# Two heads' outputs in the spare rows of the others: an output projection on three and a half row tiles instead of four

## The chip, the cores and the metric

One Trainium2 chip, one of its cores. The metric is the device time of one execution in microseconds (us); the kernel before took 1962.9 us (median of three runs, 1961.62 to 1962.97).

## The reference

Two kinds of layers alternate, twice each, on x of shape 1 x 2048 x 448 in float32:

```python
def _A_ref(x, wq, wk, wv, wo):        # attention, 16 heads of 28, one key and value for all heads
    q = (x @ wq).reshape(B, S, H, Dh).transpose(0, 2, 1, 3)
    k = x @ wk
    v = x @ wv
    scores = jnp.einsum("bhqd,bkd->bhqk", q, k) * (Dh ** -0.5)
    p = _softmax(scores, axis=-1)
    o = jnp.einsum("bhqk,bkd->bhqd", p, v)
    return o.transpose(0, 2, 1, 3).reshape(B, S, H * Dh) @ wo

def _B_ref(x, w_gate, w_up, w_down):  # feed-forward, F = 1792
    return (_silu(x @ w_gate) * (x @ w_up)) @ w_down

x = x + _A_ref(_layernorm(x), ...)
x = x + _B_ref(_layernorm(x), ...)
x = x + _A_ref(_layernorm(x), ...)
x = x + _B_ref(_layernorm(x), ...)
```

The change lies in the last product of `_A_ref`, (2048 x 448) @ (448 x 448), and in the hand-over from the first `_B_ref` to the second `_A_ref`.

## The kernel before

**Tiles.** The residual x stays in SBUF as `xres`, 16 tiles of 128 rows. The 2048 rows are worked on in four chunks of 512 (c = 0 to 3). Operands of most products are cut in a high and a low part (`split`: high on POOL by a rounding copy, low as the rest), and a product is made of three: high by high, high by low, low by high.

**Attention.** `GR` lists 16 passes i, one for each chunk c and group g of four heads, and each pass has 16 key tiles kt, so the loop in `Attention.scores` runs n = 16 i + kt over 256 steps. `step(n)` makes the scores of four heads at once, on four row strips of the array, 32 rows each (28 of them a head's own): three heads into three banks of PSUM (`three`), the fourth into one of the banks 6 and 7 (`one`, chosen by `single`). ScalarE makes the exponentials (L638 to L644); in odd steps the fourth head goes through a copy on VectorE (L640). After each odd step `pv` multiplies the two steps before by the values and VectorE adds into an accumulator (L679, L682).

**Layout of a group's output.** The four heads of a group lie one above the other, 32 rows each: 28 of the head's own, one with the sum of its softmax, three of zeros. So a group fills 128 rows and only 112 carry output.

**Post-processing.** Three pairs of steps after a pass has ended, at kt = 5 of the next pass, `rest` runs: VectorE takes the reciprocal of the sums, SyncE writes it to DRAM and reads it back spread over the rows (L703, L704), POOL multiplies (L711) and splits into `onh` and `onl` (L139, L140 in the helper `split`).

**Output projection.** When the fourth group of chunk 0, 1 or 2 is done, `between`, called after each odd step, runs `outproj` at the next kt = 10: for each of the chunk's four row tiles 4 groups x 3 products of full height (L614), then one addition into `xres` on VectorE (L618). Tiles 0 and 1 use two of the three banks in `free`, tiles 2 and 3 banks 6 and 7. The last chunk's projection is made after the loop, between two units of the feed-forward. `load_wo(z)`, at kt = 8 of passes 2 and 3, loads the output weights in the same layout: 28 rows of 32 for each head, the other four cleared by POOL.

**What else runs in passes 4c + 5.** The table `later` puts the next layernorm of a chunk into the pass that follows its projection: four statistics at kt 0 to 3, the reciprocal root on POOL at kt 4 (L246, L247), then per row tile one application (L255) and one transposition (L260) on VectorE; the transposed chunk goes to DRAM and comes back through `load`. At kt = 8 of passes 11 to 13 the weights of the first feed-forward blocks are loaded into the tile `wr` and split on POOL; `wr` has one buffer, which `load_wo` uses too.

**Order.** Each engine works through its instructions in the order in which the program issues them, SyncE's transfers and POOL's operations among them (`manual_schedule`), so a waiting instruction holds back all behind it on its engine.

**Hand-over.** In the last feed-forward block of layer 0, `hand_over` prepares the next attention. Chunk 0 is normalised, sent to DRAM and loaded back transposed into `xn`, a tile with one buffer, and `cut` splits it. Chunk 1's `ready` applies its norm into the same `xn`; it is queued by `soon` behind three calls of `project`. TensorE then transposes it (`flip`, L296). `unit` runs the lists in `mid` between its matmuls, those in `soon` near its end.

Of the kernel before, what the change touches and what calls it, by code (L numbers as in the profile page):

```python
# [52 lines left out]
def forward(  # L53
# [84 lines left out]
    def split(hi, lo, raw):  # L138
        nc.gpsimd.tensor_scalar(hi, raw, 1.0, 0.0, ALU.mult, ALU.add)  # L139
        nc.gpsimd.tensor_tensor(lo, raw, hi, ALU.subtract)  # L140
# [93 lines left out]
    def norm_steps(c, away=None, n=1):  # L234


        got = {}

        def stat(t):
            nc.vector.bn_stats(stats[:, 4 * c + t, :], xres[:, 4 * c + t, :])  # L240
            nc.vector.bn_aggr(mv[:, 4 * c + t, :], stats[:, 4 * c + t, :])

        def scale(z):
            m = 4 // n
            rstd = pers.tile([P, 4], F32, name="rstd", bufs=2)[:, 0:m]
            nc.gpsimd.tensor_scalar(rstd, mv[:, 4 * c + m * z : 4 * c + m * z + m, 1], 1.0, EPS, ALU.mult, ALU.add)  # L246
            nc.gpsimd.tensor_tensor(rstd, rstd, halfn[:, 0:m], ALU.pow)  # L247
            got["r"] = got.get("r", []) + [rstd[:, t : t + 1] for t in range(m)]

        def apply(t):  # L250
            if t == 0:
                got["x"] = pers.tile([P, 4, 512], F32, name="xn")
            got["o"] = (away() if away else got["x"][:, t, :])[:, 0:D]
            i, r = xres[:, 4 * c + t, :], got["r"][t]
            nc.vector.tensor_scalar(got["o"], i, mv[:, 4 * c + t, 0:1], r, ALU.subtract, ALU.mult)  # L255
            if not away:
                nc.gpsimd.tensor_copy(got["x"][:, t, D:512], got["o"][:, 384:D])

        def turn(t):
            nc.vector.transpose(side()[:, :, :, t], got["o"].rearrange("p (k s) -> p k s", s=32))  # L260

        def side():
            return got["x"].rearrange("p t n -> p (t n)")[:, 0 : 4 * D].rearrange("p (k s t) -> p k s t", s=32, t=4)

        def send():
            turns.append(dram.tile([D, 512], F32, name=f"xt{len(turns)}"))
            got["xt"] = turns[-1]
            for a in range(4):
                nc.sync.dma_start(
                    got["xt"].rearrange("(k r) n -> r k n", r=32)[:, :, P * a : P * a + P],  # L270
                    side()[32 * a : 32 * a + 32].rearrange("p k s t -> p k (s t)"),
                )

        def load():
            got["raw"] = pers.tile([P, 4, 512], F32, name="xn")
            rows3(got["raw"], got["xt"])

        got["load"] = load
        fs = [lambda t=t: stat(t) for t in range(4)] + [lambda z=z: scale(z) for z in range(n)]
        for t in range(4):  # L280
            fs += [lambda t=t: apply(t)] + [lambda t=t: turn(t)] * bool(away)
        return fs + [send] * bool(away), got
# [3 lines left out]
    def cut(got, tiles, ks=range(4), copy=nc.scalar.copy):  # L286

        for k in ks:
            flipped(tiles, k, got["raw"][:, k, :], copy)

    def flip(got, tiles, ks=range(4)):

# [68 lines left out]
    class Attention:  # L361
# [230 lines left out]
        def scores(self, ff):  # L592
            next(switch)
            with tc.tile_pool(name=f"at{self.layer}", bufs=1, reuse_waits="tile") as wp:
# [3 lines left out]
                todo, due = [], {}  # L598
                single = lambda d: banks[6 + d % 2]

                def load_wo(z):
                    r = wpool.tile([P, 4, 2, P], F32, name="wr").rearrange("p (z k) b n -> p z (k b n)", z=2)
                    nc.gpsimd.memset(r, 0.0)
                    for j in range(4):
                        nc.sync.dma_start(r[32 * j : 32 * j + DH, :, 0:D], wos[j][:, 2 * z : 2 * z + 2, :])
                    zs = slice(2 * z, 2 * z + 2)
                    split(woh[:, zs, :], wol[:, zs, :], r[:, :, 0:D])

                def outproj(c, t, po, gs=range(NG)):
                    oh, ol = on[c]  # L610
                    ts_ = slice(P * t, P * t + P)
                    for g in gs:
                        for z, (a, b) in enumerate(((oh, woh), (oh, wol), (ol, woh))):
                            nc.tensor.matmul(  # L614
                                po[:, 0:D], a[:, g, ts_], b[:, g, :], start=(g + z == 0), stop=(g == NG - 1 and z == 2)
                            )
                    if gs[-1] == NG - 1:
                        return lambda: nc.vector.tensor_tensor(  # L618
                            xres[:, 4 * c + t, :], po[:, 0:D], xres[:, 4 * c + t, :], ALU.add
                        )  # L620
# [26 lines left out]
                def between(d):  # L647

                    i, kt = divmod(2 * d, NT)
                    free, one = threes[0], single(d + 1)  # L650
                    if full:
                        self.lent = free[:, 0, :]
                        if 6 <= kt < 14:
                            self.advance(min(NM // 4, NM * (i + 2) - self.done))
                        if kt == 14 and i + 1 < len(GR):
                            self.places[i + 1](free[:, 1, :])
                    if not todo or kt != 10:
                        return
                    c = todo.pop()
                    for f in [outproj(c, t, free[:, t, :]) for t in range(2)]:  # L660
                        f()
                    outproj(c, 2, one)()
                    outproj(c, 3, single(d))()

                def pv(d):

# [19 lines left out]
                def post(i):  # L686

                    c, g = GR[i]
                    out2 = accs.pop(i)
                    oraw, rb = out2[:, 0, :], out2[:, 1, :]  # L690
                    rs = wp.tile([P, 16], F32, name="rs", bufs=2)
                    for j in range(4):
                        nc.sync.dma_start(rs[32 * j : 32 * j + 32, :], oraw[32 * j + DH : 32 * j + DH + 1, :])

                    def rest():
                        if fine is not None:
                            under = wp.tile([P, 16], F32, name="under", bufs=2)
                            for bound, op in ((LIMIT, ALU.is_lt), (1.0 / LIMIT, ALU.is_gt)):
                                nc.vector.tensor_scalar(under, rs, bound, None, op)
                                nc.vector.tensor_tensor(fine, fine, under, ALU.mult)  # L700
                        nc.vector.reciprocal(rs, rs)
                        rd = dram.tile([4, 512], F32, name="rd", bufs=2)
                        nc.sync.dma_start(rd.rearrange("j (p n) -> (j p) n", n=16), rs)  # L703
                        nc.sync.dma_start(rb, rd[:, None, :].to_broadcast([4, 32, 512]))  # L704
                        if g == 0:
                            on[c] = (
                                wp.tile([P, NG, 512], F32R, name="onh"),
                                wp.tile([P, NG, 512], F32R, name="onl"),
                            )
                        oh, ol = on[c]  # L710
                        nc.gpsimd.tensor_tensor(rb, oraw, rb, ALU.mult)  # L711
                        split(oh[:, g, :], ol[:, g, :], rb)
                        if g == NG - 1 and c < NC - 1:
                            todo.append(c)

                    return rest
# [16 lines left out]
                for n in range(last):  # L733
# [5 lines left out]
                    if kt == 12 and i + 2 < len(GR):  # L739
                        self.stack(i + 2)  # L740
                    if i in (2, 3) and kt == 8:
                        load_wo(i - 2)
                    if n == NT and ff.nxt:
                        ff.nxt.below(nc.sync)
                    if kt == 8 and 10 < i <= 11 + FG:
# [37 lines left out]
    class FeedForward:  # L783
# [251 lines left out]
        def hand_over(self, gi, c):  # L1035

            a = self.nxt
            fs, got = norm_steps(c, None if c else lambda: qraw)
            for f in fs[:5]:
                f()  # L1040
            a.pool = self.stage
            a.X[c] = xtile(xpool if c < 2 else self.xbp)

            def ready():
                for f in fs[5:]:
                    f()
                a.norms[c] = got

            wipe = lambda: nc.gpsimd.memset(qraw, 0.0)
            if c == 0:  # L1050
                self.soon.append([1, lambda: [f() for f in fs[5:9]]])
                self.soon.append([2, lambda: [f() for f in (*fs[9:], got["load"], wipe)]])
                self.mid[gi, 3, 1] = [lambda: None, lambda: cut(got, a.X[c])]
                self.soon.append([5, lambda: [a.project() for _ in range(3)]])
            elif c == 1:
                self.soon.append([3, ready])
            else:
                a.plan[4 * c - 4, 0] = [ready]

# [254 lines left out]
```

## Time and profile before

| | |
|---|---|
| median of three runs | 1962.9 us (1961.62 to 1962.97) |
| profiled execution, its own time | 1962.7 us |
| its span (first to last instruction) | 1960.9 us |
| granted TensorE clock | 1.00 |
| TensorE matmuls, busy | 1947.1 us, 99% |
| VectorE / ScalarE / GpSimd, busy | 1016.9 / 1339.3 / 771.3 us |
| DMA | 79.69 MB, mean 41 GB/s |
| matmuls of the output projection (L614) | 384, of which 288 in the six projections inside the loop |

In the rows below PE is TensorE's matmuls, PEld its weight loads, DVE VectorE, ACT ScalarE, POOL GpSimd, SP SyncE; SPq is a transfer issued from SyncE's queue. A row of a timeline has the start in us, the time taken, engine, line, operation, the tiles written and read, and how many were merged into the row; in brackets how long the engine had been idle before it and what ended that. A row of several merged instructions spans from the first's start to the last's end.

### The profile page before, as it was taken

What the parts mean: (1) busy time and instruction counts of PE and PEld (TensorE: products, weight loads), DVE (VectorE), ACT (ScalarE), POOL (GpSimd) and SP (SyncE); (2) the same over time, 40 slices, a digit from 0 to 9 for tenths busy, and PEclk for the clock granted to TensorE, in tenths of its full rate; (3) what the DMA queues carried; (4) which work ended last, traced back from release to release, by engine and by line L of the source; (5) the groups of instructions that cost most, each with busy time, mean ns of one, the idle gap of its engine ahead of it and who ended that gap; (6) DMA issues with size and microseconds to landing.
All of it is one profiled execution on the core that took longest, in us unless ns stands there. A gap on an engine that the chain in (4) does not pass through costs nothing. (4 is left out here: it accounts for less than half of the span.)

```text
span 1960.9 us, 45644 instructions
## 1 busy us (share of the span) xinstructions
PE 1947.1 (99%) x18307; PEld 1319.9 (67%) x18307; DVE 1016.9 (52%) x1711; ACT 1339.3 (68%) x2353; POOL 771.3 (39%) x997
## 2 busy tenths in 40 slices
PE   9999999999999999999999999999999999999998
PEld 8544545445458999999974444454444688999997
DVE  7434543544435567665654335435444346667653
ACT  4899797998964344444349998979979533444432
POOL 5212111132314868766341221111222167688640
PEclk9999999999999999999999999999999999999999
DMA  5111020121210110011131111102112101110102
GB/s 168 53 30 26 25 49 20 32 59 28 73 33 2 53 33 24 24 33 27 52 112 33 29 31 31 45 12 61 31 50 50 33 6 49 33 32 22 27 17 77
DMA packets 100001, 79.69 MB, mean 41 GB/s; under 512 B 26024, under 2 KB 82984, under 8 KB 99784
## 3 DMA queue, kind: packets, MB, share of 16 engines
q1 hardware_dynamic: 99208, 75.81, 14.3%
q8 instruction: 144, 2.36, 0.5%
q10 hardware_dynamic: 576, 0.92, 0.1%
q14 instruction: 73, 0.60, 0.1%
HBM read 57.15 MB, written 18.74 MB: 39 GB/s over the span
## 5 line engine op out<-in xcount | busy, mean ns | idle before, releaser
L672 PE MATMUL bank<-pt,vsb 128*32 128x512 f32 x4096 | 493.3, 598 | 0.3
L631 PE MATMUL bank<-qstack,keys 32*128 32x512 f32 x1536 | 484.7, 425 | 0.0
L631 PE MATMUL three<-qstack,keys 32*128 32x512 f32 x4608 | 460.6, 425 | 1.5 <-DVE vt L565 1.2
L631 PEld LDWEIGHTS three<-qstack,keys 32*128 32x128 f32 x4608 | 254.4, 182 | 295.0 <-ACT pt L644 179.4
L638 ACT ACTIVATE pt<-three 128x1536 f32<-128x1536 f32 x256 | 372.1, 1454 | 1.2 <-PE bank L672 0.8
L644 ACT ACTIVATE pt<-three 128x1536 f32<-128x1536 f32 x256 | 371.7, 1452 | 0.0
L350 PE MATMUL bank<-xh,wgh 64*128 64x512 f32 x1344 | 364.5, 392 | 0.3 <-DVE sg L1111 0.3
L350 PE MATMUL bank<-wdh,h 64*128 64x448 f32 x1776 | 329.4, 364 | 0.1
L640 DVE COPY raw<-bank 128x512 f32<-128x512 f32 x256 | 177.2, 692 | 226.9 <-PE bank L631 224.6
L350 PE MATMUL bank<-xh,wgl 64*128 64x512 f32 x1020 | 291.8, 390 | 0.0
L682 DVE TENSOR_TENSOR o<-bank,o 128x512 f32<-128x512 f32 x224 | 154.9, 691 | 239.5 <-PE bank L672 234.6
L672 PEld LDWEIGHTS bank<-pt,vsb 128*32 128x32 f32 x4096 | 107.1, 109 | 249.7 <-issue 153.0
L711 POOL TENSOR_TENSOR o<-o 128x512 f32<-128x512 f32 x32 | 41.2, 1287 | 592.6 <-DMA o<-rd 459.3
L357 ACT COPY seen<-bank 128x1 f32<-128x1 f32 x788 | 100.2, 163 | 243.4 <-PE bank L350 182.4
L350 PE MATMUL bank<-xl,wgh 64*128 64x512 f32 x912 | 254.9, 390 | 0.0
L631 PEld LDWEIGHTS bank<-qstack,keys 32*128 32x128 f32 x1536 | 243.4, 183 | 1.2 <-DVE o L682 0.6
L350 PEld LDWEIGHTS bank<-wdh,h 64*128 64x128 f32 x1776 | 237.7, 184 | 9.5 <-issue 2.0
L350 PE MATMUL bank<-wdl,h 64*128 64x448 f32 x888 | 213.2, 366 | 0.0
L350 PEld LDWEIGHTS bank<-xh,wgh 64*128 64x128 f32 x1344 | 200.3, 184 | 11.6 <-DVE sg L1111 0.7
L897 POOL TENSOR_TENSOR xres<-stage,xres 128x448 f32<-128x448 f32 x120 | 151.0, 1269 | 113.0 <-ACT stage L890 112.8
L643 ACT ACTIVATE pt<-bank 128x512 f32<-128x512 f32 x256 | 151.0, 590 | 61.1 <-PE bank L631 60.9
L862 DVE TENSOR_TENSOR xn<-bank,xn 128x512 f32<-128x512 f32 x192 | 126.5, 687 | 125.7 <-PE bank L350 94.7
(202 smaller groups left out, 3085.3 us busy)
## 6 DMA issues: line engine op xcount, KB each, us to landing
o<-rd SPq DMA_DIRECT2D x32, 256.0 KB
qraw<-qd SPq DMA_DIRECT2D x128, 56.0 KB
qd<-stage SPq DMA_DIRECT2D x30, 224.0 KB
xt<-xn SPq DMA_DIRECT2D x28, 224.0 KB
wdr<-in_B_w_down_dram SPq DMA_DIRECT2D x28, 224.0 KB
wr<-in_B_w_gate_dram SPq DMA_DIRECT2D x32, 192.0 KB
wr<-in_B_w_up_dram SPq DMA_DIRECT2D x32, 192.0 KB
xn<-xt SPq DMA_DIRECT2D x7, 768.0 KB
```

The lines of the kernel that those rows point to most:

```text
L350: nc.tensor.matmul(po, a, b, start=start, stop=stop, skip_group_check=True)
L357: nc.scalar.copy(seen[:, i : i + 1], po[:, 0:1])
L631: nc.tensor.matmul(three[:, j, :] if j < 3 else one, k[js, kp, ks], q[js, part, :], start=(z == 0), stop=(z == 2), tile_position=(32 * j, 0),)
L638: nc.scalar.activation(pt, three, AF.Exp, scale=SCALE)
L640: nc.vector.tensor_copy(raw, one)
L643: nc.scalar.activation(pt1, one, AF.Exp, scale=SCALE)
L644: nc.scalar.activation(pt, three, AF.Exp, scale=SCALE)
L672: nc.tensor.matmul(po[32 * j : 32 * j + 32, :], vsb[:, n % NT, :], pts[n][j], start=(n == 2 * d), stop=(n > 2 * d), skip_group_check=True,)
L682: nc.vector.tensor_tensor(acc, in_turn(po), acc, ALU.add)
L711: nc.gpsimd.tensor_tensor(rb, oraw, rb, ALU.mult)
L862: plus = lambda out, po, r: tt(by_tile(out), in_turn(po), by_tile(r), ALU.add)
L897: nc.gpsimd.tensor_tensor(r, h[e, t], r, ALU.add)
```

## The change

Heads 14 and 15 are the third and fourth head of the last group. Their 56 output rows are 14 times four rows, and the other 14 heads have four spare rows each. The change moves them there:

- `on[c]` becomes one tile that holds high and low part side by side. After the fourth group's split, `spread` issues 14 transfers inside SBUF, each of four rows (both parts, 4 KB a row) into the spare rows of one head, and then one that copies rows 0 to 63 of the fourth group over rows 64 to 127, where heads 14 and 15 had been.
- `dense` makes the projection of two row tiles: three groups at full height for each, then three pairs of half height, one tile's on rows 0 to 63, the other's on 64 to 127. It runs twice, at kt = 14 instead of 10.
- `load_wo` has two forms. The dense one puts rows of heads 14 and 15 of the weights into the spare rows, and needs no clearing; it is loaded where the old one was. The old one is loaded for the last chunk, at kt = 2 of passes 13 and 14.
- At the hand-over, chunk 0 is loaded back into the tiles of the keys 2 and 3 instead of `xn`, in four transfers instead of three, and chunk 1's `ready` follows chunk 0's `cut` directly, in front of the three projections.

```diff
-        def load():
-            got["raw"] = pers.tile([P, 4, 512], F32, name="xn")
-            rows3(got["raw"], got["xt"])
+        def load(into=None):
+            if into is None:
+                got["raw"] = pers.tile([P, 4, 512], F32, name="xn")
+                rows3(got["raw"], got["xt"])
+                return
+            two, one = (t.bitcast(F32) for t in into)
+            nc.sync.dma_start(two, got["xt"][0:256, :].rearrange("(k p) n -> p k n", p=P))
+            nc.sync.dma_start(one[:, 0], got["xt"][256:384, :])
+            for rs in (slice(0, 64), slice(64, 128)):
+                nc.sync.dma_start(one[rs, 1], got["xt"][384:448, :])
+            got["apart"] = [two[:, 0], two[:, 1], one[:, 0], one[:, 1]]
...
-                def load_wo(z):
+                def load_wo(z, dense):
                     r = wpool.tile([P, 4, 2, P], F32, name="wr").rearrange("p (z k) b n -> p z (k b n)", z=2)
-                    nc.gpsimd.memset(r, 0.0)
+                    if not dense:
+                        nc.gpsimd.memset(r, 0.0)
+                    spare = wo[14 * DH : 16 * DH, :].rearrange("(q r) n -> r q n", r=4)
                     for j in range(4):
-                        nc.sync.dma_start(r[32 * j : 32 * j + DH, :, 0:D], wos[j][:, 2 * z : 2 * z + 2, :])
+                        for up in (0, 64) if dense and z and j < 2 else (0,):
+                            own = slice(2 * z + bool(up), 2 * z + (1 if dense and z and j > 1 else 2))
+                            to = slice(bool(up), own.stop - 2 * z)
+                            p0 = up + 32 * j
+                            nc.sync.dma_start(r[p0 : p0 + DH, to, 0:D], wos[j][:, own, :])
+                            if dense:
+                                qs = slice(4 * own.start + j, 4 * own.stop - 3 + j, 4)
+                                nc.sync.dma_start(r[p0 + DH : p0 + 32, to, 0:D], spare[:, qs, :])
                     zs = slice(2 * z, 2 * z + 2)
                     split(woh[:, zs, :], wol[:, zs, :], r[:, :, 0:D])
+                def spread(o):
+                    for q in range(14):
+                        p0 = 64 + 4 * q + 4 * (q > 6)
+                        dma(o[32 * (q % 4) + DH : 32 * (q % 4) + 32, q // 4], o[p0 : p0 + 4, 3])
+                    dma(o[64:128, 3], o[0:64, 3])
+
+                def dense(c, ts, pos):
+                    o = on[c]
+                    cols = [slice(P * t, P * t + P) for t in ts]
+                    terms = ((0, woh), (0, wol), (1, woh))
+                    for cs, po in zip(cols, pos):
+                        for g in range(3):
+                            for z, (v, b) in enumerate(terms):
+                                nc.tensor.matmul(
+                                    po[:, 0:D], o[:, g, v, cs], b[:, g, :], start=(g + z == 0), stop=False, skip_group_check=True
+                                )
+                    side_by_side(
+                        *(
+                            [(po[:, 0:D], (o[rs, 3, v, cs], b[rs, 3, :]), False, z == 2) for z, (v, b) in enumerate(terms)]
+                            for cs, po, rs in zip(cols, pos, HALVES)
+                        )
+                    )
+                    for t, po in zip(ts, pos):
+                        x = xres[:, 4 * c + t, :]
+                        nc.vector.tensor_tensor(x, po[:, 0:D], x, ALU.add)
...
-                    if not todo or kt != 10:
+                    if not todo or kt != 14:
                         return
                     c = todo.pop()
-                    for f in [outproj(c, t, free[:, t, :]) for t in range(2)]:
-                        f()
-                    outproj(c, 2, one)()
-                    outproj(c, 3, single(d))()
+                    dense(c, (0, 1), (free[:, 0, :], free[:, 1, :]))
+                    dense(c, (2, 3), (one, single(d)))
...
                         nc.gpsimd.tensor_tensor(rb, oraw, rb, ALU.mult)
-                        split(oh[:, g, :], ol[:, g, :], rb)
+                        split(o[:, g, 0, :], o[:, g, 1, :], rb)
                         if g == NG - 1 and c < NC - 1:
+                            spread(o)
                             todo.append(c)
...
                     if i in (2, 3) and kt == 8:
-                        load_wo(i - 2)
+                        load_wo(i - 2, True)
+                    if i in (13, 14) and kt == 2:
+                        load_wo(i - 13, False)
...
-                self.soon.append([2, lambda: [f() for f in (*fs[9:], got["load"], wipe)]])
+                self.soon.append([2, lambda: [f() for f in (*fs[9:], lambda: got["load"](keys[2:4]), wipe)]])
                 self.mid[gi, 3, 1] = [lambda: None, lambda: cut(got, a.X[c])]
                 self.soon.append([5, lambda: [a.project() for _ in range(3)]])
             elif c == 1:
-                self.soon.append([3, ready])
+                self.mid[gi, 3, 1].append(ready)
```

More of the change, by code (lines that the diff above doesn't have):

```diff
@@ L288, in cut @@
         for k in ks:
-            flipped(tiles, k, got["raw"][:, k, :], copy)
+            flipped(tiles, k, got["apart"][k] if "apart" in got else got["raw"][:, k, :], copy)
     def flip(got, tiles, ks=range(4)):
@@ L609, in outproj @@
                 def outproj(c, t, po, gs=range(NG)):
-                    oh, ol = on[c]
+                    oh, ol = (on[c][:, :, v, :] for v in range(2))
                     ts_ = slice(P * t, P * t + P)
@@ L705, in rest @@
                         if g == 0:
[L706 to L710, printed above, removed]
+                            on[c] = wp.tile([P, NG, 2, 512], F32R, name="on")
+                        o = on[c]
                         nc.gpsimd.tensor_tensor(rb, oraw, rb, ALU.mult)
-                        split(oh[:, g, :], ol[:, g, :], rb)
+                        split(o[:, g, 0, :], o[:, g, 1, :], rb)
                         if g == NG - 1 and c < NC - 1:
+                            spread(o)
                             todo.append(c)
```

## The prediction

> **What bounds the kernel now.** I read the head of the page first, then the table of windows, then the timelines of single engines around the output projections, in that order, because the head of the page does not say which engine sets the pace.
>
> ```profile
> span 1960.9 us, 45644 instructions
> PE 1947.1 (99%) x18307; PEld 1319.9 (67%) x18307; DVE 1016.9 (52%) x1711; ACT 1339.3 (68%) x2353; POOL 771.3 (39%) x997
> ```
>
> TensorE (PE) is busy throughout, but its matmul ends are modelled, so 99% cannot be taken at its word. The table of windows has, for each stretch, busy time of each engine with its number of instructions, then the granted clock. The first row below is an output projection in layer 1, the second twelve pairs of plain attention steps:
>
> ```profile
> 1172.70:1183.00 10.30, 10.30 (x56) 9.00 (x52) 2.47 (x4) 1.42 (x2) 1.13 (x1) 1.00 0.01 2
> 1361.40:1405.70 44.30, 44.30 (x484) 18.66 (x488) 21.09 (x37) 44.30 (x49) 12.19 (x16) 1.00 0.26 66
> ```
>
> In plain steps ScalarE (ACT, fourth) is busy for all 44.30 us: the exponentials follow one another without a hole. In the output projection it works 1.42 us of 10.30. The clock is 1.00 in both. ScalarE's timeline gives the beat, from one L643 to the next:
>
> ```profile
> 1460.82 0.59 ACT L643 ACTIVATE pt<-bank 128x512 f32<-128x512 f32 x1
> ...
> 1462.64 1.45 ACT L638 ACTIVATE pt<-three 128x1536 f32<-128x1536 f32 x1
> ...
> 1464.51 0.59 ACT L643 ACTIVATE pt<-bank 128x512 f32<-128x512 f32 x1
> ```
>
> Two steps take 3.69 us (1464.51 - 1460.82). So in attention ScalarE is the bound, and an output projection counts in full, since ScalarE starves through it. The rows of PE, ScalarE and VectorE (DVE) around the first one show it:
>
> ```profile
> 200.70 0.47 PE L614 MATMUL three<-woh,onh 128*128 128x448 f32 x1
> 201.01 0.36 PE L614 MATMUL three<-wol,onh 128*128 128x448 f32 x1
> ...
> 210.33 0.37 PE L614 MATMUL bank<-woh,onl 128*128 128x448 f32 x1
> 210.62 0.51 PE L631 MATMUL three<-qstack,keys 32*128 32x512 f32 x3
> ...
> 211.69 0.60 ACT L643 ACTIVATE pt<-bank 128x512 f32<-128x512 f32 x1 [9.70 <-PE bank L631]
> ...
> 210.73 0.62 DVE L618 TENSOR_TENSOR xres<-bank,xres 128x448 f32<-128x448 f32 x1 [1.81 <-PE bank L614]
> ```
>
> The hole in ScalarE is 9.70 us, and from the second to the last of the 48 matmuls a new one starts every (210.33 - 201.01) / 46 = 0.203 us. Whatever shortens or lengthens this stretch of PE shows in the time one for one. It happens six times (three chunks, two layers).
>
> **Fewer matmuls.** Each projection goes from 48 full matmuls to 36, and 6 pairs on half the rows. That pairs of half height run side by side is seen in the feed-forward part:
>
> ```profile
> 1703.99 0.42 PE L350 MATMUL bank<-wdh,h 64*128 64x448 f32 x2
> ...
> 1705.01 0.42 PE L350 MATMUL bank<-wdh,h 64*128 64x448 f32 x2
> 1705.21 0.39 PE L350 MATMUL bank<-mixed,wgh 64*128 64x512 f32 x1
> ```
>
> From 1703.99 to 1705.21 lie six pairs of the same width: 0.203 us a pair, as much as one full matmul. So 42 slots stand for 48: 6 x 0.203 = 1.2 us each, **-7.2 us** in six.
>
> The array changes its split more often: before, into full height and out of it (2 changes); now full, halves, full, halves, out (5). The first matmul after a change takes 201.01 - 200.70 = 0.31 us, 0.11 over the beat; the way out, 210.62 - 210.33 = 0.29, is 0.09 over. Three more at 0.1, six times: **+1.8 us**. [...]
>
> **The last additions.** Before, the third row tile's addition ran while PE made the fourth tile, and only the fourth tile's came after PE. The two now end together. The next attention step needs, for its fourth matmul, the bank of the third tile (bank 6 both at key tile 12 before and at key tile 0 now). VectorE begins 0.40 us after the last matmul's start (210.73 - 210.33) and takes 0.62, so that matmul can start 1.02 after it instead of 0.29: **0.7 us** more each, +4.2 us in six. Nothing hides it, since ScalarE already waits for just these scores.
>
> **Spreading two heads.** After the low parts of the last group are split on POOL, SyncE (SP) issues 14 small transfers inside SBUF, waits until all have landed (the last copy overwrites their source), and issues that copy. No such transfer is in the trace; the nearest rows are these (xN merges N issues):
>
> ```profile
> 200.45 1.29 POOL L140 TENSOR_TENSOR onl<-o,onh 128x512 fp32r<-128x512 f32 x1
> ...
> 191.42 0.35 SPq L703 DMA_DIRECT2D rd<-rs  x1
> 192.84 0.56 SPq L704 DMA_DIRECT2D o<-rd  x1
> ...
> 1512.23 2.45 SPq L693 DMA_DIRECT2D rs<-o  x4
> ...
> 576.53 1.18 SPq L124 DMA_DIRECT2D xd<-xh  x2
> ...
> 142.10 0.95 POOL L603 MEMSET wr<- 128x1024 f32 x1
> 147.01 0.94 POOL L139 TENSOR_SCALAR woh<-wr 128x896 fp32r<-128x896 f32 x1 [3.95 <-ACT pt L643]
> ...
> 143.09 1.65 SPq L605 DMA_DIRECT2D wr<-in_A_wo_dram  x4
> ```
>
> Call T the end of the low split, 200.45 + 1.29 = 201.74, which is 1.04 after the old projection's start. Issue interval: inside SBUF 2.45 / 4 = 0.61 and 1.18 / 2 = 0.59; from DRAM 1.65 / 4 = 0.41. I take 0.585, near the kind that is alike, bounds 0.41 to 0.61. From a small transfer's issue to one that waits for it: 192.84 - 191.42 = 1.42; the new ones issue 0.2 longer, so 1.6. For the large copy the bounds are that 1.42 and, from the four loads of weights, 147.01 - 143.09 - 3 x 0.41 = 2.7; its 256 KB are nearer the loads: 2.4. With 0.1 for the hand-over: 0.1 + 13 x 0.585 + 1.6 + 2.4 = T + 11.7.
>
> The projection is moved by two pairs of steps, to T - 1.04 + 2 x 3.69 = T + 6.3, and needs the copy after 18 full matmuls (3.65): T + 10.0. So PE stands 1.7 us (0 to 2.1 by the interval) in five of the six: +8.5. The sixth, in layer 1, is late already:
>
> ```profile
> 1429.65 0.47 PE L614 MATMUL three<-woh,onh 128*128 128x448 f32 x1
> ...
> 1433.41 0.47 PE L614 MATMUL three<-woh,onl 128*128 128x448 f32 x1 [0.68 <-POOL onl L140]
> ...
> 1442.32 0.60 ACT L643 ACTIVATE pt<-bank 128x512 f32<-128x512 f32 x1 [11.38 <-PE bank L631]
> ```
>
> There ScalarE starves 11.38, which is 1.7 over the 9.70 of the first: that stall goes, **-1.7**. Low parts came about 3.7 after the start; since the weight loads that shared the DMA engines with the normaliser now queue behind the spreading, I put it between 1.04 and 3.7, at 2.2, and the new stall at 1.7 + 1.2 = 2.9. Spreading in all: **+11.4 us**.
>
> **What queues behind it.** In each layer's third chunk the loads of a feed-forward block stand on SP behind the spreading, and in front of POOL's next jobs; the old form of the output weights is now loaded again just there, ahead of the norm's reciprocal root. SP, POOL, then VectorE:
>
> ```profile
> 1423.60 0.47 SPq L127 DMA_DIRECT2D wr<-in_B_w_gate_dram  x1
> ...
> 1425.33 0.58 SPq L127 DMA_DIRECT2D wr<-in_B_w_up_dram  x1
> ...
> 1432.08 1.27 POOL L140 TENSOR_TENSOR onl<-o,onh 128x512 fp32r<-128x512 f32 x1
> ...
> 1439.65 0.67 POOL L140 TENSOR_TENSOR wdl<-wdr,wdh 128x224 fp32r<-128x224 f32 x1
> 1446.60 0.62 POOL L139 TENSOR_SCALAR qstack<-qraw 128x512 fp32r<-128x512 f32 x1 [6.28 <-PE bank L631]
> 1447.30 1.28 POOL L140 TENSOR_TENSOR qstack<-qraw,qstack 128x512 fp32r<-128x512 f32 x1
> ...
> 1456.05 1.01 POOL L247 TENSOR_TENSOR rstd<-rstd,halfn 128x4 f32<-128x4 f32 x1
> ...
> 148.03 2.12 POOL L140 TENSOR_TENSOR wol<-wr,woh 128x896 fp32r<-128x896 f32 x1
> ...
> 1441.36 0.62 DVE L618 TENSOR_TENSOR xres<-bank,xres 128x448 f32<-128x448 f32 x1 [1.86 <-PE bank L614]
> ...
> 1458.56 0.50 DVE L255 TENSOR_SCALAR sg<-xres,mv,rstd 128x448 f32<-128x448 f32 x1
> 1459.83 0.69 DVE L682 TENSOR_TENSOR o<-bank,o 128x512 f32<-128x512 f32 x1 [0.76 <-ACT pt L644]
> ```
>
> The copy is issued at T + 9.3; the first weight load at T + 9.9 (before: at 1423.60, 9.8 before T); the first of w_up 1.7 later and landed 2.4 after that, T + 14.0; twelve splits take 1440.32 - 1433.35 = 7.0, T + 21; the queries' split 2.0, T + 23; clearing 0.95, T + 23.9; loads 3.95, T + 27.9; two splits 3.1, T + 31; the root about 1.2: T + 32.2. VectorE wants it for L255. Before, L255 came 17.2 after the last addition (1458.56 - 1441.36), of which 7.4 were two pairs of steps that now lie ahead. After the copy PE has three pairs, 18 full matmuls and three pairs, with the changes 5.0 us to the start of the last, T + 16.7, the addition 0.4 later, so L255 is due at T + 17.1 + 9.8 + 0.7 = T + 27.6. VectorE stands 4.6 us, with its accumulation behind it (L682, which frees the bank for the next scores). That had 0.76 to spare, and ScalarE has up to one step in hand (1462.64 - 1460.82 = 1.8): 2.0 to 3.8 are lost, I take 2.7, **+5.4 us** for two layers.
>
> **First chunk into key tiles.** The second chunk's normalisation no longer queues for the one buffer and moves ahead of three projections:
>
> ```profile
> 986.90 2.91 PE L296 MATMUL bank<-ident,xn 128*128 128x128 f32 x16 [2.09 <-DVE xn L255]
> ...
> 986.27 1.85 DVE L255 TENSOR_SCALAR xn<-xres,mv,rstd 128x448 f32<-128x448 f32 x4
> ```
>
> PE idles 2.09 there, and its 16 transposes go at VectorE's pace; with the four done early I take **-2.5** (bounds 2.1 and 2.9). Its price, VectorE 1.85 us earlier in that unit, lies beside the projections; without that cover it would be 1.85.
>
> The denser loads of the output weights (8 and 12 instead of 4 a half, no clearing) lie in stretches where POOL idles: nothing; without that cover 12 x 0.41 = 4.9 us of SP.
>
> **Sum.** -7.2 + 1.8 + 4.2 + 11.4 - 1.7 - 2.5 + 5.4 = +11.4. The profiled execution took 1962.7 us (span 1960.9 and 1.8 around it), 0.2 under the median of 1962.9; so 1962.9 + 11.4 = **1974.3 us**. By the terms' bounds alone: 1966 to 1985.
>
> **Rivals.** A difference of 0.2% (3.9 us) is about what can be told from none.
> (1) Spreading in time. Below an issue interval of (10.0 - 0.1 - 1.6 - 2.4) / 13 = 0.45 us PE doesn't wait; at 0.41 the stalls go (-11.4, the late sixth keeps about 0.9) and POOL's queue costs 4.6: 1962.9 - 7.2 + 1.8 + 4.2 + 0.9 - 1.7 - 2.5 + 4.6 = 1963.0. For: loads from DRAM. Against: both kinds inside SBUF.
> (2) Spreading in time, and POOL's queue short enough for L255 as well (it takes 4.6 us less for any reason, such as weights that land sooner): 1957.5, faster.
> (3) The 14 transfers wait for one another, if the kept order takes their rows as shared: 14 x 1.6 + 2.5 = T + 24.9, a stall of 14.9, six times in place of 11.4: about 2052. Against: the four L693, which write one tile, run at 0.61, under the 1.42 of a wait.
> (4) The halves don't run side by side here, as they read one tile: 6 x 6 x 0.203 = 7.3 more, 1981.6. Against: the pairs of L350 read one tile too.
>
> **How the numbers follow.** Forecast 0.55, (1) 0.17, (2) 0.20, (3) 0.05, (4) 0.03. Slower is forecast, (3) and (4): 0.63; same is (1): 0.17; faster is (2): 0.20. The range, 1956 to 1988, takes in all but (3) and the ends of the others; the likeliest case alone has 1966 to 1985.
>
> **What would show it.** ScalarE's hole at each projection: 9.70 before, 9.70 - 1.2 + 0.3 + 0.7 + 1.7 = 11.2 forecast, 9.5 under (1) and (2). PE idle before the first paired matmul, released by a transfer inside SBUF. L255 of the third chunk's norm behind a POOL root that ended late. The wait of 2.09 before L296 gone. The forecast is wrong if the hole falls below 9.7 or L255 doesn't wait.

## The result and the profile after

The changed kernel takes 1999.38 us (median of six runs, 1996.24 to 2001.94) against 1962.51 before (also of six): ratio 1.0189, 95% interval 1.0179 to 1.0200, or 36.9 us slower. The forecast was slower by 11.4, the range ended at 1988. The direction was right, the size was not.

The head of the page and three groups of it (line numbers are those of the changed kernel: L639 and L358 the full and the halved matmuls of the projection, L674 scores, L681 to L687 exponentials, L723 the accumulation):

```profile
span 1999.3 us, 45868 instructions
PE 1960.1 (98%) x18307; PEld 1310.1 (66%) x18307; DVE 1021.2 (51%) x1711; ACT 1339.2 (67%) x2353; POOL 786.9 (39%) x1005
...
L674 PE MATMUL bank<-qstack,keys 32*128 32x512 f32 x1536 | 484.9, 425 | 12.7 <-DVE o L723 10.2
...
L681 ACT ACTIVATE pt<-three 128x1536 f32<-128x1536 f32 x256 | 372.3, 1454 | 15.0 <-PE bank L713 14.6
...
L686 ACT ACTIVATE pt<-bank 128x512 f32<-128x512 f32 x256 | 151.5, 592 | 86.9 <-DVE stats L240 84.3
```

The work is the same, 18307 matmuls and 1339 us of ScalarE; what grew is idle time. ScalarE's 84.3 us ahead of L686 are the six holes at the projections (60.3 before). The name behind the arrow, a statistic on VectorE, is only the last thing to end before the scores did; the rows below show PE itself late. The 14.6 us ahead of L681 and PE's 10.2 on L723 are new: both are the accumulation that came late in the passes after the third chunks.

ScalarE's hole at each projection, from the timelines, in us:

| kernel | layer 0: chunk 0, 1, 2 | layer 1: chunk 0, 1, 2 | elsewhere in attention |
|---|---|---|---|
| before | 9.70, 9.70, 9.70 | 9.89, 9.89, 11.38 | none over 0.4 |
| after | 14.64, 14.22, 15.31 | 14.31, 12.97, 12.81 | 8.28, 6.93 in passes 13 |
| forecast | 11.2, 11.2, 11.2 | 11.2, 11.2, 12.4 | 2.7, 2.7 |

The holes account for +24.0 us and passes 13 for +15.2 (7.42 and 0.86, 6.45 and 0.48); the time between the last exponential of layer 0 and the first of layer 1 fell by 2.8 (468.5 to 465.7). That places 36.4 us of the 38.4 by which the span of the profiled execution grew (1960.9 to 1999.3); that execution was one of the longer ones.

The first projection, row by row: POOL's last split, SyncE's 15 transfers, PE, VectorE and ScalarE.

```profile
200.48 1.29 POOL L140 TENSOR_TENSOR on<-o,on 128x512 fp32r<-128x512 f32 x1
...
201.79 11.10 SPq L124 DMA_DIRECT2D on<-on  x15
...
208.33 0.47 PE L639 MATMUL three<-woh,on 128*128 128x448 f32 x1
...
211.10 0.44 PE L639 MATMUL three<-woh,on 128*128 128x448 f32 x1 [1.29 <-DMA on<-on]
...
215.44 0.47 PE L358 MATMUL three<-woh,on 64*128 64x448 f32 x1 [1.23 <-DMA on<-on]
...
216.75 0.94 PE L639 MATMUL bank<-woh,on 128*128 128x448 f32 x2
217.48 0.58 PE L639 MATMUL bank<-wol,on 128*128 128x448 f32 x1
...
222.14 0.37 PE L358 MATMUL bank<-woh,on 64*128 64x448 f32 x2
222.44 0.50 PE L674 MATMUL three<-qstack,keys 32*128 32x512 f32 x3
223.22 0.49 PE L674 MATMUL bank<-qstack,keys 32*128 32x512 f32 x1 [0.27 <-DVE xres L650]
...
224.26 0.60 ACT L686 ACTIVATE pt<-bank 128x512 f32<-128x512 f32 x1 [14.64 <-DVE stats L240]
```

PE stands twice for the spread rows, at the third group and at the pairs, and the first pair is complete only from 215.44, 3.3 us after it could have been (208.33 + 18 x 0.203 + 0.2). Then something that no step of mine had: from 216.75 two matmuls take 217.48 - 216.75 = 0.73 us, 0.37 each, where 0.203 was the beat. The table of windows gives the reason in the column of the granted clock:

```profile
211.00:216.70 5.70, 4.37 (x20) 3.29 (x21) 0.28 (x1) 0.00 (x0) 0.00 (x0) 1.00 0.36 91
216.80:220.10 3.30, 3.30 (x11) 2.95 (x9) 0.77 (x2) 0.00 (x0) 1.90 (x2) 0.50 0.00 0
```

At the end stands the wait that was forecast: the fourth score matmul at 223.22, held by the third tile's addition (L650).

The other loss, in pass 13 of layer 0 (SyncE, POOL, VectorE, ScalarE, then windows; the first row of POOL is the low split that the spreading follows):

```profile
494.64 2.47 SPq L734 DMA_DIRECT2D rs<-o  x4
497.21 3.04 SPq L619 DMA_DIRECT2D wr<-in_A_wo_dram  x4
...
466.32 1.28 POOL L140 TENSOR_TENSOR on<-o,on 128x512 fp32r<-128x512 f32 x1
...
493.61 0.95 POOL L612 MEMSET wr<- 128x1024 f32 x1
502.37 0.94 POOL L139 TENSOR_SCALAR woh<-wr 128x896 fp32r<-128x896 f32 x1 [7.81 <-PE bank L674]
...
505.83 1.02 POOL L247 TENSOR_TENSOR rstd<-rstd,halfn 128x4 f32<-128x4 f32 x1
...
506.88 0.51 DVE L255 TENSOR_SCALAR sg<-xres,mv,rstd 128x448 f32<-128x448 f32 x1 [6.74 <-POOL rstd L247]
...
511.67 1.45 ACT L681 ACTIVATE pt<-three 128x1536 f32<-128x1536 f32 x1 [7.42 <-PE bank L713]
...
500.00:507.00 7.00, 2.46 (x27) 0.81 (x19) 0.26 (x2) 4.25 (x5) 4.22 (x4) 0.99 0.12 32
507.00:513.70 6.70, 5.65 (x29) 1.93 (x33) 4.01 (x11) 1.97 (x2) 0.00 (x0) 0.50 0.18 49
```

VectorE stands 6.74 us at L255 for the root, as forecast in kind. But the reload's transfers were issued at 497.21, behind the four L734 of SyncE's queue, though POOL had cleared their tile by 494.56; and the clock is at 0.50 while PE catches up.

### The profile page after: what moved, and what is told of

It reads as the page before. It is cut to its first block, busy times and chain, and to the rows that moved or that the text cites. A ratio compares the mean times of both kernels' runs of the same rounds, so it can differ in the third digit from the quotient of the medians.

```text
span 1999.3 us, 45868 instructions
## 1 busy us (share of the span) xinstructions
PE 1960.1 (98%) x18307; PEld 1310.1 (66%) x18307; DVE 1021.2 (51%) x1711; ACT 1339.2 (67%) x2353; POOL 786.9 (39%) x1005
## 5 line engine op out<-in xcount | busy, mean ns | idle before, releaser
L674 PE MATMUL bank<-qstack,keys 32*128 32x512 f32 x1536 | 484.9, 425 | 12.7 <-DVE o L723 10.2
L674 PE MATMUL three<-qstack,keys 32*128 32x512 f32 x4608 | 463.8, 426 | 1.5 <-DVE vt L573 1.2
L674 PEld LDWEIGHTS three<-qstack,keys 32*128 32x128 f32 x4608 | 254.6, 183 | 295.3 <-ACT pt L687 177.7
L681 ACT ACTIVATE pt<-three 128x1536 f32<-128x1536 f32 x256 | 372.3, 1454 | 15.0 <-PE bank L713 14.6
L687 ACT ACTIVATE pt<-three 128x1536 f32<-128x1536 f32 x256 | 372.1, 1453 | 0.0
L358 PE MATMUL bank<-xh,wgh 64*128 64x512 f32 x1344 | 356.8, 392 | 0.3 <-DVE sg L1152 0.3
L358 PE MATMUL bank<-wdh,h 64*128 64x448 f32 x1776 | 324.2, 364 | 0.1
L358 PE MATMUL bank<-xh,wgl 64*128 64x512 f32 x1020 | 287.4, 390 | 0.0
L723 DVE TENSOR_TENSOR o<-bank,o 128x512 f32<-128x512 f32 x224 | 154.8, 691 | 240.7 <-PE bank L713 237.3
L749 POOL TENSOR_TENSOR o<-o 128x512 f32<-128x512 f32 x32 | 41.2, 1287 | 578.2 <-DMA o<-rd 457.9
L674 PEld LDWEIGHTS bank<-qstack,keys 32*128 32x128 f32 x1536 | 244.8, 183 | 18.2 <-DVE o L723 11.6
L358 PE MATMUL bank<-xl,wgh 64*128 64x512 f32 x912 | 249.2, 390 | 0.0
L358 PEld LDWEIGHTS bank<-wdh,h 64*128 64x128 f32 x1776 | 225.9, 184 | 10.7 <-issue 2.0
L686 ACT ACTIVATE pt<-bank 128x512 f32<-128x512 f32 x256 | 151.5, 592 | 86.9 <-DVE stats L240 84.3
L358 PE MATMUL bank<-wdl,h 64*128 64x448 f32 x888 | 205.1, 366 | 0.0
L358 PEld LDWEIGHTS bank<-xh,wgh 64*128 64x128 f32 x1344 | 192.5, 184 | 13.3 <-issue 1.1
```

What stands on the lines that cost most here:

```text
L358: nc.tensor.matmul(po, a, b, start=start, stop=stop, skip_group_check=True)
L674: nc.tensor.matmul(three[:, j, :] if j < 3 else one, k[js, kp, ks], q[js, part, :], start=(z == 0), stop=(z == 2), tile_position=(32 * j, 0),)
L681: nc.scalar.activation(pt, three, AF.Exp, scale=SCALE)
L686: nc.scalar.activation(pt1, one, AF.Exp, scale=SCALE)
L687: nc.scalar.activation(pt, three, AF.Exp, scale=SCALE)
L723: nc.vector.tensor_tensor(acc, in_turn(po), acc, ALU.add)
```

## The experiments

All ratios are to the kernel before, run on the same chip beside them.

**The hand-over alone.** The kernel before, with the edits of `load`, `cut` and `hand_over` only.

> The kernel before with the hand-over edit alone (first chunk loaded back into the key tiles, second chunk's norm ahead of the projections). Theory: this part is independent of the rest and gives what the profile after shows between the last exponential of layer 0 and the first of layer 1, about -2.8 us (1959.7). Rival: the gain belongs to the shifted schedule of the whole change; alone it gives nothing (within 1 us of before).

1958.93 us, ratio 0.9982 (0.9973 to 0.9991). PE's timeline at the transposes:

```profile
984.82 1.47 PE L304 MATMUL bank<-ident,xn 128*128 128x128 f32 x12
986.55 0.63 PE L304 MATMUL bank<-ident,xn 128*128 128x128 f32 x4 [0.26 <-DVE vt L573]
```

They start where the projection ends, without the 2.09 us of before. This part is a gain by itself, 3.7 us here, of which the interval holds 1.8 to 5.3; the theory's 2.8 lies inside. In the profile the time between the layers falls by 2.9, and the late sixth hole is 10.42 instead of 11.38.

**The reload one pass later.**

```diff
-                    if i in (13, 14) and kt == 2:
-                        load_wo(i - 13, False)
+                    if i in (14, 15) and kt == 2:
+                        load_wo(i - 14, False)
```

> The changed kernel with the second load of the output weights one pass later (passes 14 and 15 instead of 13 and 14). Theory: VectorE's wait for the reciprocal root in passes 13 comes from POOL's queue, and without the reload ahead of it the holes of 7.4 and 6.5 us in ScalarE (15.2 us in all with what follows them) go: about 1984. Rival: the weight splits that start late behind the spreading hold the root up on their own: 1997 to 2000, the holes stay.

1985.55 us, ratio 1.0120 (1.0104 to 1.0135). Passes 13 have no hole left; the root's row has no late predecessor now, it waits for its own input:

```profile
493.82 0.20 POOL L246 TENSOR_SCALAR rstd<-mv 128x4 f32<-128x4 f32 x1 [1.60 <-DVE mv L241]
...
487.76 0.60 ACT L686 ACTIVATE pt<-bank 128x512 f32<-128x512 f32 x1 [13.09 <-DVE stats L240]
```

The holes at the projections stay (12.6 to 13.1, one 15.65 with a halved clock). So 14 us of the loss hang on where the reload stands.

**The projection two pairs later.** On top of that:

```diff
-                    if not todo or kt != 14:
+                    if not todo or kt != 2:
...
-                    n = NT * (4 * c + 5)
+                    n = NT * (4 * c + 5) + 6
```

> The kernel of the run before it, with the dense projection two pairs of steps later still (key tile 2 of the next pass) and the norm that follows moved by six steps. Theory: with the spreading landed before PE comes, both waits inside the projection and the halved clock behind them go; ScalarE's holes fall from 12.8 to 15.3 us to about 9.5, in all 1962.5 - 2.8 - 7.2 + 1.8 + 4.2 - 1.7 = 1957 us. Rival: the cost sits in the spreading's traffic and in SyncE's blocked queue, not in where the projection stands: holes stay over 12 us, about 1980.

2006.49 us, ratio 1.0229 (1.0215 to 1.0243): a miss in the sum. ScalarE, POOL and VectorE in the pass after the first projection:

```profile
226.79 0.60 ACT L686 ACTIVATE pt<-bank 128x512 f32<-128x512 f32 x1 [9.92 <-PE bank L674]
247.67 1.45 ACT L681 ACTIVATE pt<-three 128x1536 f32<-128x1536 f32 x1 [4.17 <-PE bank L713]
...
238.11 1.29 POOL L749 TENSOR_TENSOR o<-o 128x512 f32<-128x512 f32 x1 [19.13 <-DMA o<-rd]
...
241.84 1.01 POOL L247 TENSOR_TENSOR rstd<-rstd,halfn 128x4 f32<-128x4 f32 x1
...
242.88 0.51 DVE L255 TENSOR_SCALAR sg<-xres,mv,rstd 128x448 f32<-128x448 f32 x1 [3.50 <-POOL rstd L247]
```

The six holes fell to 9.8 to 9.9, as the theory of late rows has it. But my shift by six steps put the root behind L749, which waits on POOL for the normaliser; with twelve weight splits in between, the third chunks' holes there were 11.5 and 12.2 us. In sum the holes away from the projections are 43 us, twice the 21 that the projections gained on the run before.

**Halves first in the second half.** On top of that, for row tiles 2 and 3 the pairs come ahead of the full matmuls, and each tile's addition follows its own last matmul.

> The kernel of the run before it, with the pairs of half height made first for the third and fourth row tile and each tile's addition right behind its last matmul. Theory: the third tile's bank is free when the next scores want it (0.7 us each) and one change of the array's split goes (0.1): six times 0.8, about 4.8 us below the run before. Rival: the next scores do not wait for that bank but for something else of the same length: no change (within 1 us).

2002.17 us, ratio 1.0204 (1.0190 to 1.0218). Holes at the projections 8.9, 0.95 less than in the run before; the time fell by 4.3. The wait for the third tile's addition was real.

**Filling the waits.** The changed kernel, with spare matmuls where PE stood:

```diff
+                    spare = threes[0][:, 2, 0:D]
+                    def fill(k):
+                        for _ in range(k if ts[0] == 0 else 0):
+                            nc.tensor.matmul(spare, o[:, 0, 0, 0:P], woh[:, 0, :], start=True, stop=True, ...)
...
+                            if g == 2 and po is pos[0]:
+                                fill(6)
...
+                    fill(6)
                     side_by_side(
```

> The changed kernel with 12 matmuls more in each dense projection, six ahead of the third group of the first row tile and six ahead of the first pairs of half height, into a bank that nobody reads: TensorE works where it stood idle for transfers. The results stay the same. Theory: the halved clock (3.4 us at a time, in four of the six projections of the profile after) comes from TensorE's idle time just before; with it filled no projection has a halved clock and each hole in ScalarE is about 12.8 to 13.0 us (the added 2.4 us lie inside the waits): about 6 us less than the changed kernel, 1993. Rival: the clock falls for another reason and the matmuls only add their time: 2005 to 2014.

1997.58 us, ratio 1.0174 (1.0160 to 1.0188), against 1.0189 for the changed kernel: the intervals overlap, so the forecast 6 us did not show in the time. The mechanism did show in the windows at the same place:

```profile
211.00:216.00 5.00, 4.91 (x25) 3.97 (x24) 0.00 (x0) 0.00 (x0) 0.00 (x0) 1.00 0.38 94
216.00:220.60 4.60, 4.60 (x25) 3.79 (x24) 1.16 (x2) 0.00 (x0) 1.93 (x2) 1.00 0.03 10
```

The clock is 1.00 at all six projections, with 12 matmuls more in each, and the holes are 12.6 to 14.1, in sum 79.6 against 84.3. Only passes 13, which were not filled, keep a halved clock. In the profiles of the four runs with all 14 transfers on SyncE at this place and no filling (the changed kernel, the reload late, and the two runs that follow), 11 of 24 projections have a halved clock. How many meet it differs between executions: the mean clock of the changed kernel's six runs goes from 0.992 in the longest (2001.94 us) to 0.996 in the shortest (1996.24), so most of the spread of 5.7 us goes with it. In the five runs here it is 0.995 or 0.996.

**Weights ahead of the spreading.** The changed kernel, feed-forward weights of pass 12 at key tile 2:

```diff
-                    if kt == 8 and 10 < i <= 11 + FG:
+                    if kt == (2 if i == 12 else 8) and 10 < i <= 11 + FG:
```

> The changed kernel with the feed-forward weights of pass 12 loaded at key tile 2 instead of 8, so that they stand on SyncE ahead of the spreading. The reload stays in pass 13. Theory: POOL's queue in pass 13 then holds only the reload ahead of the root; the chain is shorter by the 12 splits and the late loads (about 11 us), so the root comes in time and the holes of 7.4 and 6.5 us go: about 1985. Rival: the reload alone, by its clearing, its loads and its splits (8 us), keeps the root late: holes of 3 us or more stay, over 1992.

2001.99 us, ratio 1.0201 (1.0186 to 1.0217): no gain, holes of 6.7 and 6.3 stay in passes 13. This struck down the chain of my prediction. POOL and SyncE:

```profile
498.56 0.94 POOL L139 TENSOR_SCALAR woh<-wr 128x896 fp32r<-128x896 f32 x1 [15.71 <-DMA wr<-in_A_wo_dram]
...
491.54 2.47 SPq L734 DMA_DIRECT2D rs<-o  x4
494.11 2.37 SPq L619 DMA_DIRECT2D wr<-in_A_wo_dram  x4
```

POOL had cleared the tile by 482.85 and waited 15.7 us for the reload's transfers. SyncE issued these right behind L734, which waits for the end of the pass before: between 478.3 and 491.54 SyncE issued nothing. The rival's numbers came, but of the work that it named only the loads were late, and they by their place in the queue, not by their length.

**The reload ahead of L734.** On top of that, `load_wo(..., False)` at key tile 0 instead of 2.

> The kernel of x6 (feed-forward weights of pass 12 loaded early, reload in passes 13 and 14) with the reload issued at key tile 0 instead of 2, so that its four transfers stand on SyncE ahead of the four L734 that wait for the end of the pass before. Theory: what kept the root late in x6 is this place in SyncE's queue (the split of the weights waited 15.7 us for them); ahead of L734 the loads are done before the root is asked for and the holes of 6.3 and 6.7 us go: about 1986. Rival: the reload's own work on POOL (clearing and two splits, 4 us) keeps the root late wherever its transfers stand: holes over 2.5 us stay, 1992 or more.

1985.31 us, ratio 1.0111 (1.0095 to 1.0126). SyncE and POOL:

```profile
485.86 1.63 SPq L619 DMA_DIRECT2D wr<-in_A_wo_dram  x4
496.09 2.47 SPq L734 DMA_DIRECT2D rs<-o  x4
...
489.65 0.94 POOL L139 TENSOR_SCALAR woh<-wr 128x896 fp32r<-128x896 f32 x1 [3.82 <-PE bank L639]
...
498.71 0.20 POOL L246 TENSOR_SCALAR rstd<-mv 128x4 f32<-128x4 f32 x1 [5.92 <-DVE mv L241]
```

The transfers go 10 us ahead of L734, POOL is idle 5.92 us before the root, and passes 13 have no hole. Pass and work on POOL are those of the run before; the reload stands earlier on both queues, but on POOL it had only been waiting. The holes at the projections are no shorter for it (13.4 to 17.5, four with a halved clock). The reload ahead of L734 without the early weights was not run.

**The norm later still.** The run with halves first, the norm 12 steps later instead of 6.

> The kernel of x4 with the norm moved by 12 steps instead of 6, so that its reciprocal root is not issued behind the post-processing of the same pass on POOL (the multiplication waits there for the normaliser's transfer, and in pass 13 twelve weight splits follow). Theory: the holes of 2.4 to 12.9 us at the first application go, those at the projections stay at 8.9: 1962.7 - 3.7 (hand-over) - 6 x 0.85 - 1.0 = 1953. Rival: any place of the norm near the projection meets another wait on POOL or VectorE: 1965 or more.

1964.47 us, ratio 1.0006 (0.9997 to 1.0015). The holes at the first application shrank to 1.6 and 3.9 in the third chunks and went elsewhere, those at the projections are 8.9; some smaller ones follow in the passes 14. Nearer the rival: in pass 13 the root still stood behind the twelve weight splits and the split of the queries, which kept POOL busy from 495.8 to 504.7, and VectorE waited 1.89 us for it. I did not follow the rest further.

**Two queues.** The run with the late reload, with every second small transfer issued from POOL:

```diff
-                        dma(o[32 * (q % 4) + DH : 32 * (q % 4) + 32, q // 4], o[p0 : p0 + 4, 3])
+                        (nc.gpsimd if q % 2 else nc.sync).dma_start(
+                            o[32 * (q % 4) + DH : 32 * (q % 4) + 32, q // 4].bitcast(F32), o[p0 : p0 + 4, 3].bitcast(F32)
+                        )
```

> The kernel of x2 (reload late) with every second one of the 14 transfers issued from POOL's queue instead of SyncE's. Theory: what makes the copy late is the interval of 0.62 us between issues on one queue; with seven on each the last lands about 4 us earlier, both waits inside the projection go and the holes fall from 13 to about 10: 1985.5 - 18 = 1967. Rival: the transfers themselves, not their issue, take the time, or POOL's issue is as slow as all 14 on SyncE: holes stay at 12.5 or more, 1983 to 1990.

1961.88 us, ratio 0.9997 (0.9988 to 1.0006), 24 us below the 1.0120 of the same kernel with one queue, and 5 below the forecast. SyncE, POOL, PE and ScalarE:

```profile
202.17 4.42 SPq L629 DMA_DIRECT2D on<-on  x7
209.34 0.53 SPq L124 DMA_DIRECT2D on<-on  x1
...
202.45 3.85 POOL L629 DMA_DIRECT2D on<-on  x7 [0.30 <-POOL on L140]
...
212.41 0.76 PE L358 MATMUL three<-woh,on 64*128 64x448 f32 x2
...
213.01 0.36 PE L358 MATMUL three<-woh,on 64*128 64x448 f32 x1
...
213.22 0.36 PE L358 MATMUL three<-woh,on 64*128 64x448 f32 x1
...
219.99 0.60 ACT L688 ACTIVATE pt<-bank 128x512 f32<-128x512 f32 x1 [10.13 <-DVE stats L240]
```

Seven issues take 4.42 us on SyncE, 0.63 each, while POOL makes the other seven; the copy is issued 7.2 us after the first of the transfers (209.34 - 202.17), where one queue took 10.6 (11.10 less the copy's own 0.53). PE hardly stands for it any more: the first pair is 0.76 us long instead of 0.47, because its second half, on the copied rows, starts 0.3 us late. All holes are 9.9 to 10.1. On one queue the issues were the larger part of that time: from the first to the fourteenth 8.2 of the 10.6 us.

**Both together.** That kernel, with halves first.

> The kernel of x8 (reload late, 14 transfers over two queues) with the pairs of half height first for the third and fourth row tile, as in x4. Theory: holes of 9.0 instead of 9.9, so 5 us below x8: 1957, and below the hand-over edit alone (1958.9), since each projection is then 0.7 us shorter than before. Rival: with the projection at key tile 14 the copy lands no earlier than the pairs need it, so the order within the second half changes nothing: 1961 to 1963.

1955.41 us, ratio 0.9960 (0.9947 to 0.9974): faster than both, 7.8 us below before. ScalarE and VectorE:

```profile
219.92 0.60 ACT L704 ACTIVATE pt<-bank 128x512 f32<-128x512 f32 x1 [8.94 <-PE bank L692]
...
217.14 0.63 DVE L652 TENSOR_TENSOR xres<-bank,xres 128x448 f32<-128x448 f32 x1 [1.40 <-PE bank L659]
218.96 0.62 DVE L652 TENSOR_TENSOR xres<-bank,xres 128x448 f32<-128x448 f32 x1 [1.19 <-PE bank L659]
```

The third tile's addition ends at 217.8, over a microsecond before the projection does, and the hole is 8.94 where 9.70 was. Against the hand-over alone (0.9982) the intervals touch, so the times leave open how much the dense projection adds; by the holes it is worth 0.5 to 2.5 us each, 6.6 in six. With 2.8 for the hand-over that makes 9.4, of which the span shows 6.8 (1960.9 to 1954.1); where the other 2.6 went stays open.

## Why the prediction was right or wrong

**Right in kind.** ScalarE's bound, the count of matmuls, the changes of split and the addition's wait make a hole of 9.70 - 1.2 + 0.3 + 0.7 = 9.5 without stalls; with two queues it is 9.9, of which 0.3 is the late first pair, and 8.9 without the addition's wait. The hand-over gave 2.8 in the profile where 2.5 was put. Spreading on SyncE was the largest loss, as forecast; rivals (1) and (2) had it in time and fell, and so did (3) and (4), since issues follow at 0.62 us and the pairs run side by side (213.22 - 213.01 = 0.21 a pair with two queues, where the clock is full).

**Spreading, mis-sized.** Put at 1.7 us a projection, it is 3.3 at the pairs of the first. The 13 intervals took 8.2 instead of 7.6 us: 0.6. From the fourteenth issue to the copy's about 2.4 instead of 1.6: 0.8. The copy's landing, 215.44 less its issue, 3.1 instead of 2.4: 0.7. The hand-over from POOL took 0.02 (201.79 less 200.48 + 1.29) instead of 0.1, and PE came to the pairs 0.4 later than forecast: 2.1 - 0.1 - 0.4 = 1.6. Both latencies were borrowed from other kinds of transfer, at values that looked cautious. That makes 9.5 + 3.3 = 12.8, and holes of 12.8 and 13.0 are what the projections with a full clock show.

**The clock, missing.** Four of the six projections in the profile had a halved clock for 3.4 us, and their holes are 1.3 to 2.4 us longer than those of the other two. Half the clock for 3.4 us accounts for at most 1.7; in the longest hole (15.31) PE also waited longer for the copy:

```profile
482.39 0.47 PE L358 MATMUL three<-woh,on 64*128 64x448 f32 x1 [2.43 <-DMA on<-on]
```

No row of before could show it, because PE's longest stop there, the 2.09 us at the hand-over, left the clock at 1.00; the prediction took a stall at its own length. Filling the waits kept the clock at 1.00 (0 of 6 projections against 11 of 24), so here the idle time brings it, though not each time; in time that filling gained nothing that can be told.

**The queue behind, wrong in its chain.** Put at 5.4 us, it cost 14. The prediction led from the spreading over late feed-forward weights to POOL; with these weights early the holes stayed. What it left out is L734: the step that places the reload's transfers at POOL's clearing forgot that they are moved behind SyncE's four L734, which wait for the end of the pass. With T = 466.32 + 1.28 = 467.60, the clearing ended at T + 27.0 instead of T + 23.9, as the late weights had it, but the reload's loads then took 7.8 us (502.37 - 494.56) instead of 3.95. The root came at 506.85, and VectorE stood 6.74 us instead of 4.6. So both chains were late here. L734 alone holds the root up, as the run with the early weights shows; the late weights alone were not run, and by these rows they would leave VectorE some 3 us (506.85 - 3.9 - 500.14, an estimate). The second error is the slack: 1.9 of 4.6 us were to be absorbed, but 8.3 of ScalarE's time went on 6.74 of VectorE's, as PE resumed at half the clock.

The terms as they came: holes +24.0 in place of +8.5 (-7.2 + 1.8 + 4.2 + 11.4 - 1.7), passes 13 +15.2 in place of 5.4, hand-over -2.8 in place of -2.5.

## What to carry to other kernels

When work moves into a chain of transfers, count the issues: here 14 of 0.62 us on one queue were a longer path than the data (8.2 us from the first issue to the last, 3.1 from the copy's issue to its landing), and a second queue was worth 24 us, three times what the whole change gave in the best kernel here (7.8). For a transfer that is added, list what stands ahead of it on its own queue and what each of those waits for, before looking at the engine that uses its data: with the early weights the reload's tile was clear by 482.85, and its transfers were issued at 494.11, behind L734. A stall of the matrix engine is priced with the clock that follows it, not by its length alone: here 0.50 for 3.4 us at four of six projections.

## What the runs showed of the hardware

The granted clock fell to 0.50 for 3.4 us (in passes 13 for 6.8) after stretches in which PE was still busy, 4.37 of 5.70 us at the first projection. The single gaps there were 0.8 to 1.3 us, once 2.4; two other projections with gaps of 0.9 to 1.3 kept it at 1.00. Only in passes 13 did PE stand still for longer than 3.4 us in one piece (5.59 and 4.62 us ahead of 508.05 and 1495.84), so no unbroken stop of that length was needed at the four projections. In the changed kernel's trace the halved stretches begin at 216.75, 349.87, 482.99, 506.88, 1210.03 and 1493.33, whole multiples of 3.413 us apart (39, 39, 7, 206 and 83). So in this trace the halved stretches begin on a beat of 3.413 us; what decides whether a stall brings one is not shown.

A transfer of 16 KB inside SBUF held SyncE's queue for 0.62 us (0.63 in the run with two queues), one of 128 KB for 0.59 (the two at 576.53 before); the issue of the 256 KB copy took 0.53 (209.34 with two queues). Seven of 16 KB on POOL took 3.85 us, 0.55 each, issued beside those on SyncE.
